# Four of twelve attention items: keys and queries turned in 64x64 tiles of TensorE, with a new order of all operations

## The chip, the core and the metric

The kernel runs on one core of one Trainium2 chip. The metric is device time in microseconds (us) of one launch, as the median of several runs; lower is better. Besides these runs one execution was recorded by the hardware profiler. All rows quoted below come from that recording, which counts time from the first instruction of the program (the span).

## The reference

Two stages follow each other. The first is a gated linear attention with a state per head, in 4 batches of 8 heads, 768 steps and a head dimension of 48:

```python
for t in range(S):
    state = alpha[:, :, t, :, None] * state + np.einsum('bhd,bhe->bhde', k[:, :, t], v[:, :, t])
    y[:, :, t] = np.einsum('bhd,bhde->bhe', q[:, :, t], state)
```

The second takes the 3072 resulting rows x (8 heads of 48 side by side, 384 numbers) through an expert layer with a hidden width of 1024: `np.maximum(x @ w1, x @ w2) @ w_out`. Inputs and output are float32.

## The kernel before

**Tiling.** The sequence is cut into 12 items of 256 steps, three to a batch (`attention(n)`, n = 0 to 11). An item holds all 8 heads, and each partition holds two neighbouring steps. The running products of alpha become sums of logarithms: `ln` (ACT), `su` (pair sums), `cs` (a matmul with a triangular matrix, L605, and sums per block, L610), and the exponentials `inv`, `en`, `ep`, `gg` on ACT. Keys and queries are scaled with these (`ka`, `kt` at L624 and L661; `qi`, `qt` at L629 and L666) into `qkt`, in float16, with a head padded to 64 columns. `vc` casts the values.

**Turning.** The score product needs keys and queries with the head dimension on the partitions. For items 0 to 7 (`TURN`) TensorE turns them: `tk` turns keys, `tq` queries, and a copy of PSUM into SBUF (`ck`, `cq`) follows on DVE or ACT (L488 and L490 are the lines of the helper `cast`). Items 8 to 11 are turned by DMA (`dk`, `dq`, L732). Where an item is not in `T64`, a turn is 8 transposes of 128x128, two heads at once (L692), and keys and queries of the item share one pair of PSUM banks. Where it is in `T64`, each 128x128 block is turned as four blocks of 64x64 that rotate over the four 64x64 tiles of the array, so a turn is 32 transposes, each with 64 columns moving, and `tk` and `tq` take a pair of banks each. Items 0 and 1 are worked in two halves of four heads.

**The rest of an item.** `kv` (L752) makes the contributions to the state in 64x64 tiles with 48 columns moving (32 matmuls; 16 in the last item of a batch). `w`, `t32` and `T` carry the state on. `sc0` and `sc1` (L832) are the scores, 16 matmuls each with 128 columns moving, `pt` masks them on DVE (L840). `yf` (12 matmuls) and `y` (56 or 60, both L877) give the output, and `xe` casts it into `xT`.

**The second stage.** It is rewritten as x @ w2 @ w_out + relu(x @ (w1 - w2)) @ w_out. So at the start `wtp` turns w2, `wd` forms w1 - w2 (DVE, L523), `woc` casts w_out, `mp` multiplies w2 by w_out, `mc` casts that product. For each group g of 256 rows there are then four `h` (6 matmuls each, L943), four relus `r` (L951 on DVE, L953 on ACT), and `o` in two parts a and b for each 128 rows (7 and 4 matmuls, L976). `ev` evicts and `st` stores. `fill` is a matmul on zeros whose result nobody reads (L419).

**What sets the order.** Every operation is an entry of a plan with durations, lags and priorities. But where the string `ORDER` is not empty, `Plan.run` returns `follow()`, which goes through the words of `ORDER`. A word names the operation, the engine (P TensorE, D VectorE, A ScalarE, G GpSimd, S the DMA queue of SyncE) and the PSUM banks:

```python
for word in ORDER.split():
    name, at = word.split(":")
    o = ops[name]
    o.eng = eng[at[0]]
```

Each engine works through its own words strictly in this order and waits where an operand isn't there. Loads go through ten buffers and SyncE's queue in the order of the string. GpSimd operations also wait for the latest VectorE operation before them in the string that is marked `port`.

Of the kernel before, what the change touches and what calls it, by code (L numbers as in the profile page):

```python
# [33 lines left out]
WP = (0.0, 0.0)  # L34
ONACT = ()
FILL = (60, 24.0)
T64 = ()
EARLY = (0, 1)
ORDER = """
fz:D setp1:G ldw20:S setd0:D fill0:P7 lda0.0:S fill31:P lda0.1:S fill32:P fill19:P ldk0.0:S fill6:P setd1:D ldq0.0:S fill5:P fill42:P mask:D fill20:P  # L40
fill38:P lda1.0:S pads0:D fill2:P ldv0.0:S fill36:P pads2:D fill28:P ln0.0:A fill17:P id32:D fill39:P wtp0.0:P6 inv0.0:A su0.0:G lda1.1:S ln0.1:A
cs0.0:P5 fill34:P ldw21:S inv0.1:A su0.1:G fill43:P wtp0.2:P4 gg0.0:A en0.0:A pads1:D fill11:P cs0.1:P ka0.0:G fill1:P fill7:P gg0.1:A fill25:P
ka0.1:D en0.1:A fill18:P kt0.0:D ep0.0:A fill37:P ldwo0:S fill24:P wtc0.0:D kt0.1:G tk0.0:P0 fill27:P wtp0.1:P6 ck0.0:D ln1.0:A qi0.0:D fill33:P
qi0.1:D fill30:P inv1.0:A qt0.0:D su1.0:G tk0.1:P ldw10:S ep0.1:A fill10:P fill8:P ck0.1:D wtc0.2:A tq0.0:P fill35:P qt0.1:D fill13:P cq0.0:A fill29:P
vc0.1:D tq0.1:P fill16:P ln1.1:A vc0.0:D sc0.0:P2 cq0.1:D ldw11:S kv0:P4 su1.1:G pt0.0:D fill22:P cs1.0:P1 fill9:P cs1.1:P gg1.0:A fill12:P en1.0:A
wtc0.1:D sc0.1:P2 ep1.0:A wtp1.1:P0 w0:D ldwo1:S gg1.1:A pt0.1:D T1.0:G fill4:P wtp1.2:P6 T1.1:G t32.1:G y0:P2 woc0.0:A ldk1.0:S w1:D woc0.1:D fill3:P
xe1:A g1:G xe0:D fill41:P wtp1.0:P5 T2.0:G wtc1.1:A ldq1.0:S mp0.1:P4 wtc1.2:A wd0.0:D mp0.2:P0 wtc1.0:A ldv1.0:S wd0.1:D h0.0:P6 en1.1:A mp0.0:P5
r0.0:A wd1.0:D h0.2:P3 lda2.0:S inv1.1:A wd1.1:D h0.4:P6 woc1.0:A lda3.0:S woc1.1:D h0.6:P2 t32.2:G ep1.1:A mp1.0:P r0.6:D r0.2:A ka1.0:G mp1.2:P
ldk2.0:S r0.4:A ka1.1:D mp1.1:P kt1.0:D mc2:A fill15:P qi1.0:D mc0:A tk1.0:P2 ldk3.0:S qi1.1:D fill14:P o0.0a:P6 qt1.0:D kt1.1:G ck1.0:A qt1.1:D
tq1.0:P fill21:P vc1.1:A tk1.1:P vc1.0:D ldq2.0:S cq1.0:D T2.1:G mc1:A kv1:P0 ck1.1:A sc1.0:P4 w2:D tq1.1:P pt1.0:D o0.0b:P T3.0:G ldq3.0:S cq1.1:A  # L50
T3.1:G ln2.0:A t32.3:D yf1:P2 sc1.1:P4 w3:D fill40:P ldv2.0:S su2.0:G inv2.0:A pt1.1:D fill26:P o0.1a:P1 ln3.0:A cs2.0:P7 ka2.0:D y1:P lda4.0:S
en2.0:A su3.0:D ep2.0:A kt2.0:G o0.1b:P xe3:D xe2:A ldv3.0:S ev0.0:D gg2.0:A cs3.0:P0 ev0.1:A h1.0:P6 ka3.0:D gg3.0:A en3.0:A ldk4.0:S tk2.0:P2
qi2.0:D h1.2:P1 r1.0:A g2:G qt2.0:D kt3.0:G inv3.0:A h1.4:P5 ldq4.0:S ep3.0:A ck2.0:D h1.6:P4 r1.2:A r1.4:D tq2.0:P qi3.0:G r1.6:A o1.1a:P1 ldv4.0:S
cq2.0:D vc2.0:A tk3.0:P4 T4.0:G qt3.0:D sc2.0:P2 t32.4:G ck3.0:A kv2:P6 o1.1b:P lda6.0:S T4.1:G w4:D pt2.0:D T5.0:G ln4.0:A tq3.0:P T5.1:G ev1.1:A
lda5.0:S o1.0a:P0 su4.0:G cq3.0:D vc3.0:A yf2:P2 sc2.1:P6 sc3.1:P4 ka4.0:G cs4.0:P1 pt2.1:D ldk5.0:S o1.0b:P en4.0:A ep4.0:A pt3.1:D y2:P ldq6.0:S
gg4.0:A ev1.0:A g4:G kt4.0:G sc3.0:P6 kv3:P4 xe4:D xe5:A ldk6.0:S pt3.0:D inv4.0:A h2.0:P0 qi4.0:G tk4.0:P2 r2.0:A w6:D h2.4:P7 ldq5.0:S t32.7:G
vc4.0:A qt4.0:D h2.2:P6 T7.0:G ln6.0:A h2.6:P0 T7.1:G w7:D ldv6.0:S ck4.0:D T8.1:G tq4.0:P r2.4:A y3:P4 T8.0:G r2.6:D cq4.0:A t32.8:G r2.2:D lda7.0:S
kv4:P0 ln5.0:A sc4.0:P2 o2.0a:P7 w8:D T9.0:D inv5.0:A ldv5.0:S T9.1:D inv6.0:A su6.0:D o2.1a:P6 t32.9:D xe7:A qi6.0:G w9:D xe6:A pt4.0:D ldq7.0:S
o2.0b:P cs6.0:P5 ev2.0:A o2.1b:P su5.0:D gg6.0:A st1.1:S ka6.0:G en6.0:A yf4:P0 ev2.1:D sc4.1:P2 ldv7.0:S h3.0:P7 ep6.0:A pt4.1:D kt6.0:G cs5.0:P6
h3.2:P4 gg5.0:A lda9.0:S r3.0:A qt6.0:D h3.4:P3 r3.2:A qi5.0:G h3.6:P7 r3.4:D vc6.0:A y4:P ldk7.0:S ka5.0:G r3.6:D en5.0:A kv6:P2 ep5.0:A xe9:D  # L60
tk6.0:P4 kt5.0:G xe8:A ldk9.0:S o3.0a:P7 qt5.0:D ck6.0:A w12:D tq6.0:P g5:G ln7.0:A st0.0:S vc5.0:G o3.0b:P cq6.0:D lda8.0:S h4.0:P6 inv7.0:A ev3.0:D
vc7.0:A tk5.0:P0 T10.0:D h4.6:P7 su7.0:D ldq9.0:S T13.0:D cs7.0:P5 t32.13:G h4.2:P4 en7.0:A t32.10:G w13:D tq5.0:P r4.0:A r4.6:D T10.1:G ldq8.0:S
o3.1a:P3 ln9.0:A qi7.0:G ck5.0:D r4.2:A cq5.0:D h4.4:P2 su9.0:G st0.1:S kv5:P6 r4.4:A sc5.0:P0 ldk8.0:S o3.1b:P w10:D gg7.0:A pt5.0:D T11.1:G ep7.0:A
o4.0a:P4 inv9.0:A T11.0:G lda10.0:S ev3.1:A ka7.0:G qt7.0:D yf5:P0 ln8.0:A sc5.1:P2 sc6.0:P6 ka9.0:G o4.0b:P pt5.1:D inv8.0:A st2.0:S o4.1a:P5 kt7.0:G
st1.0:S pt6.0:D ldv9.0:S y5:P T13.1:D kv7:P2 ldq10.0:S g7:G xe10:D xe11:A sc6.1:P6 t32.14:G o4.1b:P pt6.1:D su8.0:G h5.0:P1 ev4.1:A cs9.0:P0 w14:D
st4.1:S h5.6:P5 en9.0:A t32.15:G ldv8.0:S h5.4:P7 T15.1:G w15:D r5.6:A r5.0:D h5.2:P6 T14.0:G ev4.0:A st2.1:S kt9.0:G tk7.0:P2 r5.2:A st3.0:S cs8.0:P1
ck7.0:D tq7.0:P ep9.0:A y6:P4 en8.0:A cq7.0:D ka8.0:G ep8.0:A sc7.0:P2 r5.4:A o5.1a:P6 dk9:S T15.0:G pt7.0:D ln10.0:A qi9.0:G o5.0a:P7 gg8.0:A xe12:D
gg9.0:A vc9.0:A T14.1:G qt9.0:D kt8.0:G o5.1b:P xe13:A yf7:P2 ev5.1:A sc7.1:P4 h6.0:P0 pt7.1:D g8:G dk8:S o5.0b:P r6.0:A h6.6:P6 T16.1:D ev5.0:A
su10.0:D dq9:S h6.2:P0 vc8.0:A t32.16:G r6.6:D qi8.0:G h6.4:P7 inv10.0:A r6.2:D y7:P T16.0:G r6.4:D kv9:P4 qt8.0:D xe14:A kv8:P6 o6.0a:P0 xe15:A w18:D
dq8:S T19.0:G cs10.0:P1 t32.19:G h7.0:P3 gg10.0:A ldk10.0:S en10.0:A qi10.0:D o6.0b:P ldv10.0:S ep10.0:A w19:D T19.1:G o6.1a:P2 r7.0:A st3.1:S  # L70
qt10.0:D ev6.0:A lda11.0:S sc9.1:P4 w16:D sc9.0:P0 h7.2:P3 T17.0:G pt9.0:D ldk11.0:S T17.1:G h7.6:P7 r7.2:A o6.1b:P pt9.1:D r7.6:A ka10.0:G h7.4:P6
st4.0:S ev6.1:A yf8:P0 g10:G r7.4:D sc8.1:P2 kt10.0:G sc8.0:P4 o7.0a:P7 vc10.0:A pt8.0:D o7.1a:P6 pt8.1:D dk10:S o7.0b:P t32.20:D y8:P kv10:P2 xe16:A
xe17:D T20.1:G y9:P4 ka11.0:G ln11.0:A h8.0:P1 xe18:D ev7.0:A su11.0:G o7.1b:P inv11.0:A st7.0:S xe19:A h8.6:P7 ldq11.0:S ev7.1:D h8.2:P0 dq10:S
r8.0:D cs11.0:P6 w20:D r8.2:A h8.4:P1 r8.6:D T21.1:G en11.0:A h9.0:P0 T21.0:G r8.4:D ep11.0:A o8.1a:P7 kt11.0:D gg11.0:A h9.6:P1 T20.0:G dk11:S
qi11.0:G h9.2:P5 r9.6:A h9.4:P4 ldv11.0:S g11:G qt11.0:D t32.21:G o8.1b:P r9.4:A o8.0a:P1 w21:D ev8.1:A r9.2:D r9.0:A t32.22:D yf10:P2 sc10.1:P4
T22.1:D sc10.0:P6 dq11:S T22.0:G o8.0b:P pt10.0:D o9.0a:P0 st6.0:S pt10.1:D vc11.0:G st5.0:S o9.1a:P7 st6.1:S st5.1:S kv11:P4 y10:P w22:D st7.1:S
T23.1:G sc11.0:P4 st8.1:S o9.0b:P xe21:D xe20:A T23.0:G pt11.0:D o9.1b:P h10.0:P6 ev8.0:A ev9.1:D yf11:P2 r10.0:A sc11.1:P4 ev9.0:D h10.2:P7 pt11.1:D
st9.0:S h10.4:P6 r10.2:A h10.6:P1 y11:P r10.6:D o10.0a:P7 xe22:A xe23:D r10.4:A h11.0:P5 o10.1a:P6 r11.0:D h11.6:P5 h11.4:P4 h11.2:P3 r11.4:D o10.1b:P
r11.2:D o10.0b:P ev10.1:D o11.1a:P4 r11.6:D st10.1:S ev10.0:A o11.0a:P6 st8.0:S st9.1:S o11.1b:P o11.0b:P st10.0:S ev11.1:D o11.1c:P7 st11.1:S
ev11.0:D o11.1d:P st11.0:S ev11.11:A st11.11:S  # L80
"""
SHIFT = {}
FIX = {}
# [216 lines left out]
def kernel(  # L300
# [42 lines left out]
    A = {}  # L343
# [85 lines left out]
    def on(key):  # L429
        return "ACT" if key in ONACT else "SP"  # L430

    def add_load(n, which, prio):
# [616 lines left out]
```

## Time and profile before

| | |
|---|---|
| median of 3 runs | 139.66 us (139.44 to 139.73) |
| the profiled execution | 139.41 us, span 137.6 us |
| busy, DVE / ACT / POOL | 99.2 / 74.5 / 69.6 us |
| matmuls and weight loads | 2348 each |
| DMA | 30.76 MB, mean 223 GB/s |

Busy time is the time in which an engine's instructions cover the span; for TensorE (PE) the ends of matmuls are modelled, and matmuls overlap. So a sequence of them is best priced from start to start: the start of a group's first matmul to the start of the next group. In a timeline row the columns are start, length, engine, line, operation, operands and shapes, count, and in brackets the idle time before it with what ended it. An array form such as 64*64 is the part of the array that one matmul uses.

### The profile page before, as it was taken

The numbers are of one execution on the slowest core, as the hardware profiler recorded it, in microseconds if no ns is written. First come the engines' busy times: TensorE is split into PE (matmuls) and PEld (weight loads), VectorE is DVE, ScalarE is ACT, GpSimd is POOL, SyncE is SP. The second block draws the span as 40 slices with busy tenths as digits, with TensorE's granted clock in tenths as the row PEclk, the third lists the DMA queues.
The fourth block names the chain that finished last, engine by engine and source line by source line (L and its number), as shares of the span: only waits on it lengthen the run. The fifth ranks groups of instructions, "written<-read, shape, count | busy, mean of one in ns | idle before, by whom it ended". The sixth has DMA issues, their size and how long they took to land.

```text
span 137.6 us, 5468 instructions
## 1 busy us (share of the span) xinstructions
PE 131.2 (95%) x2348; PEld 94.0 (68%) x2348; DVE 99.2 (72%) x174; ACT 74.5 (54%) x153; POOL 69.6 (51%) x109
## 2 busy tenths in 40 slices
PE   6979989999999999999999999999999999999991
PEld 2445766566786686687867886786767776677770
DVE  7639869789887997787869757876855867575440
ACT  3166365778777779479672596634617460233010
POOL 6054250345698692797679799464545352400000
PEclk9999999999999999999999999999999999999999
DMA  4999999999999999999999999458993869910063
GB/s 89 324 261 315 378 385 332 222 259 274 261 263 257 271 252 237 270 272 254 272 280 287 305 284 161 81 108 144 311 208 100 188 129 149 348 57 5 0 229 114
DMA packets 64680, 30.76 MB, mean 223 GB/s; under 512 B 58896, under 2 KB 63120, under 8 KB 64656
## 3 DMA queue, kind: packets, MB, share of 16 engines
q1 hardware_dynamic: 64656, 30.41, 90.6%
q8 instruction: 18, 0.29, 0.9%
q14 instruction: 6, 0.05, 0.1%
HBM read 23.59 MB, written 4.72 MB: 206 GB/s over the span
## 4 chain that ended last, share of the span: by engine, by line
PE 73%; DMA 13%; SPq 8%; ACT 1%; DVE 1%; issue 1%; POOL 1%; DVEq 0%
PE PS L976 28%; PE PS L943 21%; PE PS L877 10%; DMA ldf<-in_moe_w_out_dram 9%; SPq L448 6%; PE PS L692 5%; DMA ldf<-in_v_dram 4%; PE PS L832 3%; PE PS L752 2%; SPq L470 2%; PE PS L532 2%; PE PS L605 1%; PE PS L419 1%; ACT wo L488 1%; POOL v L492 1%
## 5 line engine op out<-in xcount | busy, mean ns | idle before, releaser
L976 PE MATMUL PS<-wo,g 128*128 128x384 f16 (+1 forms) x200 | 38.3, 320 | 0.1
L943 PE MATMUL PS<-xT,wd 128*128 128x256 f16 x288 | 36.3, 273 | 0.4 <-ACT xT L488 0.2
L840 DVE TENSOR_TENSOR pt<-PS,mask 128x1024 f16<-128x1024 f32 x24 | 28.8, 1219 | 4.5 <-PE PS L832 4.3
L943 PEld LDWEIGHTS <-wd 128*128 128x128 f16 x288 | 26.8, 98 | 6.1 <-DVE wd L523 1.0
L976 PEld LDWEIGHTS <-g 128*128 128x128 f16 x200 | 18.7, 98 | 11.1 <-DVE T L787 0.5
L953 ACT ACTIVATE g<-PS 128x512 f16<-128x512 f32 x27 | 15.9, 595 | 11.9 <-PE PS L943 11.8
L661 POOL TENSOR_TENSOR qkt<-ldf,en 128x768 f16<-128x768 f32 (+1 forms) x11 | 18.3, 1666 | 3.7 <-DVE s L596 1.4
L951 DVE TENSOR_SCALAR g<-PS 128x512 f16<-128x512 f32 x21 | 14.2, 687 | 5.0 <-PE PS L943 4.7
L488 ACT CAST xT<-PS 128x384 f16<-128x384 f32 x14 | 8.0, 594 | 16.1 <-PE PS L877 15.9
L976 PE MATMUL PS<-m,xT 128*128 128x384 f16 (+1 forms) x75 | 15.9, 320 | 0.0
L787 POOL TENSOR_TENSOR T<-w,gg 48x192 f16<-48x192 f32 x20 | 10.4, 520 | 10.4 <-DVE w L812 6.2
L419 PE MATMUL PS<-fz 128*128 128x512 f16 x43 | 14.3, 440 | 1.2 <-DVE fz L416 1.2
L488 ACT COPY outs<-PS 128x384 f32<-128x384 f32 (+1 forms) x16 | 7.5, 469 | 12.4 <-PE PS L976 11.5
L588 ACT ACTIVATE loga<-ldf 128x768 f16<-128x768 f32 (+1 forms) x14 | 10.6, 754 | 5.4 <-DMA ldf<-in_alpha_dram 5.4
L666 DVE TENSOR_TENSOR qkt<-ldf,PS 128x768 f16<-128x768 f32 (+1 forms) x14 | 11.6, 833 | 2.5 <-POOL ldf L629 1.7
L624 POOL TENSOR_TENSOR ldf<-ldf 128x384 f32<-128x384 f32 (+1 forms) x10 | 9.5, 950 | 4.1 <-DMA ldf<-in_k_dram 3.3
L692 PE MATMUL PS<-ident,qkt 128*128 128x128 f16 x128 | 10.4, 219 | 0.2 <-ACT qk L488 0.2
L877 PE MATMUL PS<-pt,v 64*64 64x128 f16 x576 | 10.5, 218 | 0.0
L596 POOL TENSOR_TENSOR s<-loga 128x384 f16<-128x384 f16 (+1 forms) x9 | 6.8, 750 | 7.3 <-ACT loga L588 6.6
L812 DVE TENSOR_TENSOR w<-PS,t 112x192 f32<-112x192 f32 x16 | 5.7, 355 | 6.4 <-PE PS L752 3.5
L692 PEld LDWEIGHTS <-qkt 128*128 128x128 f16 x128 | 8.5, 98 | 2.6 <-DVE qkt L666 0.9
L877 PEld LDWEIGHTS <-v 64*64 64x64 f16 x576 | 8.5, 107 | 2.0 <-issue 1.6
(77 smaller groups left out, 184.3 us busy)
## 6 DMA issues: line engine op xcount, KB each, us to landing
ldf<-in_k_dram SPq DMA_DIRECT2D x12, 384.0 KB, 6.1
ldf<-in_q_dram SPq DMA_DIRECT2D x12, 384.0 KB, 6.5
ldf<-in_v_dram SPq DMA_DIRECT2D x12, 384.0 KB, 5.8
out_dram<-outs SPq DMA_DIRECT2D x23, 192.0 KB, 3.7
ldf<-in_alpha_dram SPq DMA_DIRECT2D x10, 384.0 KB, 5.9
ldf<-in_moe_w_dram SPq DMA_DIRECT2D x4, 768.0 KB, 7.9
ldf<-in_moe_w_out_dram SPq DMA_DIRECT2D x2, 768.0 KB, 10.0
ldf<-in_alpha_dram SPq DMA_DIRECT2D x4, 192.0 KB, 5.3
```

The lines of the kernel that those rows point to most:

```text
L419: plan.add(f"fill{i}", {"PE": 0.21}, lambda eng: nc.tensor.matmul(bank(fb), lhsT=fz[:, 0:128], rhs=fz, start=True, stop=True, skip_group_c ...
L488: nc.scalar.copy(out=out, in_=in_)
L588: nc.scalar.activation(out=A["loga", n][:, hd].rearrange("p h j d -> p (h j d)"), in_=A["ld", n, "a"][:, hd].rearrange("p h d -> p (h d)") ...
L661: e.tensor_mul(out=hjd(qkts[i3], 1)[:, hd], in0=A["ld", n, "k"][:, hd].rearrange("p h (j d) -> p h j d", j=2), in1=f.unsqueeze(2).to_broad ...
L666: nc.vector.tensor_mul(out=hjd(qkts[i3], 0)[:, hd], in0=A["ld", n, "q"][:, hd].rearrange("p h (j d) -> p h j d", j=2), in1=f.unsqueeze(2). ...
L692: nc.tensor.transpose(t[:, a, r, j, :], src[:, j, r, :], ident16)
L840: nc.vector.tensor_mul(out=t.rearrange("p u r c -> p (u r) c"), in0=A["sc", n, hf].rearrange("p u (r c) -> p (u r) c", r=2), in1=mask.rear ...
L877: nc.tensor.matmul(dst, lhsT=lhsT, rhs=rhs, start=(x, u) not in begun, stop=done and ends[x, u] == i, skip_group_check=True)
L943: nc.tensor.matmul(t[:, i], lhsT=wd16[:, s, (f + i) * 128 : (f + i + 1) * 128], rhs=xT[:, s, a0 : a0 + W], start=(s == 0), stop=(s == 2), ...
L951: nc.vector.tensor_relu(o, i)
L953: nc.scalar.activation(out=o, in_=i, func=ACTF.Relu)
L976: nc.tensor.matmul(A["op", t0, c], lhsT=lhsT, rhs=rhs, start=(part == 0 and j == 0), stop=(part == 1 and j + 1 == len(todo[1])))
```

## The change

`T64` goes from empty to items 4, 5, 6 and 7. For these four, `tk` and `tq` take the other branch of the code above, which already stands in the file, and the copies `ck` and `cq` read two half banks instead of whole ones. In the built program TensorE has 2545 matmuls instead of 2348: 192 more from the turns, and 48 fills instead of 43. `ORDER` is replaced as a whole. The lags of the loads in the plan are changed too; since `ORDER` isn't empty, no number of the plan is used.

```diff
-T64 = ()
+T64 = (4, 5, 6, 7)
...
 ORDER = """
-fz:D setp1:G ldw20:S setd0:D fill0:P7 lda0.0:S fill31:P lda0.1:S fill32:P fill19:P ldk0.0:S fill6:P setd1:D ldq0.0:S fill5:P fill42:P mask:D fill20:P
...
-xe1:A g1:G xe0:D fill41:P wtp1.0:P5 T2.0:G wtc1.1:A ldq1.0:S mp0.1:P4 wtc1.2:A wd0.0:D mp0.2:P0 wtc1.0:A ldv1.0:S wd0.1:D h0.0:P6 en1.1:A mp0.0:P5
-r0.0:A wd1.0:D h0.2:P3 lda2.0:S inv1.1:A wd1.1:D h0.4:P6 woc1.0:A lda3.0:S woc1.1:D h0.6:P2 t32.2:G ep1.1:A mp1.0:P r0.6:D r0.2:A ka1.0:G mp1.2:P
-ldk2.0:S r0.4:A ka1.1:D mp1.1:P kt1.0:D mc2:A fill15:P qi1.0:D mc0:A tk1.0:P2 ldk3.0:S qi1.1:D fill14:P o0.0a:P6 qt1.0:D kt1.1:G ck1.0:A qt1.1:D
-tq1.0:P fill21:P vc1.1:A tk1.1:P vc1.0:D ldq2.0:S cq1.0:D T2.1:G mc1:A kv1:P0 ck1.1:A sc1.0:P4 w2:D tq1.1:P pt1.0:D o0.0b:P T3.0:G ldq3.0:S cq1.1:A
...
+setp1:G lda0.0:S ln0.0:A fz:D setd0:D fill0:P7 ldk0.0:S lda0.1:S fill44:P fill8:P fill15:P ldw20:S pads0:D id32:D ldq0.0:S setd1:D fill34:P fill10:P
...
+fill42:P fill30:P fill13:P ep1.1:A xe0:A wtc1.2:A h0.0:P3 mp0.2:P5 wd0.1:D r0.0:A lda2.0:S lda3.0:S wd1.0:D wtc1.1:D wd1.1:D h0.2:P2 h0.4:P3 woc1.1:A
+h0.6:P0 r0.2:A woc1.0:D mp1.2:P ldk2.0:S ka1.1:D ka1.0:D kt1.0:D kt1.1:D mp1.1:P r0.6:A r0.4:A qi1.0:D qt1.0:D ldq2.0:S mp1.0:P mc2:A ldq3.0:S mc1:A
+tk1.0:P2 tk1.1:P qi1.1:G mc0:A o0.0a:P5 tq1.0:P qt1.1:D tq1.1:P ck1.0:D cq1.1:D vc1.1:G vc1.0:A kv1:P0 ck1.1:A cq1.0:A t32.2:G ldk3.0:S w2:D T3.1:D
+t32.3:D w3:D ln2.0:A o0.0b:P ev0.0:A sc1.0:P2 pt1.0:D ldv2.0:S o0.1a:P6 T3.0:G yf1:P0 sc1.1:P4 pt1.1:D ln3.0:A inv3.0:A lda4.0:S fill27:P su2.0:G
...
+T8.0:G ka6.0:G tk4.0:P0 y3:P4 r2.6:D ln5.0:A ep6.0:A tq4.0:P2 o2.1a:P6 xe7:A xe6:D o2.0a:P5 h3.0:P4 t32.8:D qi6.0:D qt6.0:D su5.0:G T8.1:G ck4.0:A
+vc4.0:A cq4.0:D st0.0:S ldq5.0:S vc6.0:A r3.0:A kv4:P0 sc4.0:P2 w8:D t32.9:D o2.0b:P ev2.0:A pt4.0:D T9.0:G T9.1:G o2.1b:P w9:D h3.2:P7 kt6.0:G
...
+ka5.0:D tk6.0:P2 r3.6:A r3.4:D y4:P en5.0:A su7.0:G T10.1:D kv6:P0 xe9:D st1.0:S ldq8.0:S st0.1:S o3.0a:P7 xe8:A h4.0:P5 inv7.0:A ep5.0:A ck6.0:A
+t32.10:G w12:D t32.13:D kt5.0:D o3.0b:P r4.0:A h4.2:P4 w13:D tk5.0:P0 ck5.0:A qi7.0:G ev3.0:D st3.0:S r4.2:D tq6.0:P2 cq6.0:D cs7.0:P7 en7.0:A ep7.0:A
+h4.4:P5 r4.4:A gg7.0:A T10.0:G qi5.0:G qt5.0:D vc5.0:G ldk9.0:S o3.1a:P4 st2.0:S ka7.0:D kt7.0:G qt7.0:D h4.6:P3 r4.6:A ldq9.0:S o3.1b:P kv5:P0 w10:D
+T11.0:G tq5.0:P2 ev3.1:A cq5.0:A sc6.0:P6 pt6.0:D o4.0a:P5 ln9.0:A sc5.0:P0 pt5.0:D T11.1:G yf5:P2 sc5.1:P6 o4.0b:P ev4.0:A T13.1:G inv9.0:A ln8.0:A
+lda10.0:S ldk8.0:S ldv9.0:S vc7.0:G o4.1a:P4 kv7:P0 ldq10.0:S pt5.1:D y5:P xe11:A inv8.0:A T13.0:G g7:G t32.14:G w14:D t32.15:D sc6.1:P6 o4.1b:P
...
+h8.0:P5 inv11.0:A w20:D h9.0:P0 kt11.0:G dk11:S ev7.1:A h8.2:P7 r8.2:A t32.21:G g11:G r9.0:A h9.2:P6 ep11.0:A h8.4:P4 T21.0:D st4.1:S w21:D ldv11.0:S
+r9.2:D T22.0:G h8.6:P7 r8.6:A qi11.0:G r8.0:D h9.4:P6 r9.4:A T21.1:D qt11.0:D dq11:S h9.6:P5 o8.0a:P7 r9.6:D r8.4:A sc10.0:P0 T20.1:G T20.0:G yf10:P2
...
```

Across the whole string some operations change engine as well: relus on ACT go from 27 to 34 and on DVE from 21 to 14, evictions on ACT from 16 to 20, copies of turned tiles on ACT from 7 to 9.

## The prediction

> **What bounds the kernel now.** First the totals and the slices of the page:
>
> ```profile
> PE 131.2 (95%) x2348; PEld 94.0 (68%) x2348; DVE 99.2 (72%) x174; ACT 74.5 (54%) x153; POOL 69.6 (51%) x109
> PE   6979989999999999999999999999999999999991
> PEclk9999999999999999999999999999999999999999
> PE 73%; DMA 13%; SPq 8%; ACT 1%; DVE 1%; issue 1%; POOL 1%; DVEq 0%
> ```
>
> TensorE (PE) is covered in every slice after the start, at the full granted clock, and 73% of the chain that ended last is PE; the other engines have room. Next, where the chain leaves PE:
>
> ```profile
> 11.99 12.71 DMA ldf<-in_moe_w_out_dram
> 24.72 0.84 ACT wo L488
> 25.60 2.11 PE PS L532 x12
> ```
>
> Up to 24.7 us the loads set the pace: `wo1` lands, ACT casts half of it, and mp1 starts at 25.60. From the end of mp1 (27.55) to the last matmul (134.70) the chain is nearly all PE. So I split the program at mp1. Read word by word, both orders hold the same operations of PE before mp1 and the same after it, apart from fills: five fills behind mp1 before (15, 14, 21, 40, 26), four now (27, 35, 11, 3). The part behind mp1 can then be priced as a sum.
>
> **Prices**, from start to start in the PE timeline:
>
> ```profile
> 60.87 0.86 PE L877 MATMUL PS<-pt,v 64*64 64x128 f16 x48
> 61.56 0.34 PE L877 MATMUL PS<-qk,T 48*64 48x128 f16 x12
> 61.73 0.44 PE L752 MATMUL PS<-v,qkt 64*64 64x48 f16 x32
> 62.10 0.62 PE L692 MATMUL PS<-ident,qkt 128*128 128x128 f16 x8
> 62.56 0.65 PE L976 MATMUL PS<-m,xT 128*128 128x384 f16 x3
> ```
>
> A wide turn (8 transposes) takes 62.56 - 62.10 = 0.46, in rows between wide neighbours 0.45. `y` with 60 matmuls takes 61.73 - 60.87 = 0.86. Where a wide matmul follows `y` directly (33.84 to 34.81) it is 0.97, so leaving the small tiles costs 0.11. Six `h` matmuls take 0.65 between their like and 0.74 before a small-tile group (97.52 to 98.26): entering costs 0.09. A stay in small tiles thus costs 0.20. `kv6` above takes 0.37 - 0.11 = 0.26 for 32 matmuls. With these prices the old order behind mp1 sums to 105.2 us; measured 107.15, so 1.95 are waits and misfits, 0.16 of it the pipeline's end.
>
> **The turns of items 4 to 7.** Eight turns of 0.45 go, eight turns of 32 small transposes come. No row shows these. Below: `kv6`, the same array form and rotation over four tiles with 48 columns moving, 0.26 (8.1 ns each). Above: `sc`, 128 columns moving, 16 in 0.22 (13.8 ns each), so 32 in 0.44. At 64 columns, nearest `kv`, a straight line between them gives 9.3 ns, 0.30 a turn. I take 0.30: 8 x (0.45 - 0.30) = 1.2 us saved; by the ends 1.5 or 0.1. The copies from PSUM carry as many elements as before (DVE 0.69, ACT 1.01); should the half banks halve DVE's pace, 0.7 more on four copies falls beside `o` and `h` matmuls with 0.6 us of slack (below), so I cost it at nothing, 0.1 each if that cover is gone.
>
> The Trainium skill, "TensorEngine Tiling (Array Packing)", section Instruction Overhead, speaks against this change: about 60 cycles go with each matmul, one of 1 column takes as long as one of 60, and a dimension already small is not to be tiled. Taken as 25 ns an instruction (60 cycles at the 2.4 GHz of "TensorE: Matmul & The Clock Gate") without overlap between tiles, an estimate from these pages would be 0.80 a turn and +2.8 us for the change; the row of `kv6`, 8.1 ns each, says that rotating tiles don't pay that here.
>
> **Stays in small tiles.** Counted in the strings behind mp1: 22 before, 25 now. `tk4 y3 tq4`, `tk6 y4`, `kv5 tq5 sc6`, `tk7 y6 tq7` sit beside small-tile work and cost no switch; `tk5 tq6` stands alone, `sc6`/`sc5` are parted by an `o`, and early on `kv1` and `sc1.0` are parted. +0.60 in all, 0.20 of it before the turns.
>
> **From mp1 to h2.0, the step that loses.** In the new string DVE does `wtc1.1` between the two halves of `wd1`:
>
> ```profile
> 22.64 1.83 DVE L523 TENSOR_TENSOR wd<-ldf 128x768 f16<-128x768 f32 x2 [0.24 <-DMA ldf<-in_moe_w_dram]
> 24.72 0.56 DVE L490 CAST wo<-ldf 128x768 f16<-128x768 f32 x1 [0.25 <-DMA ldf<-in_moe_w_out_dram]
> 26.06 0.36 DVE L624 TENSOR_TENSOR ldf<-ldf 128x192 f32<-128x192 f32 x1
> ```
>
> Both halves end at 24.47 here. With 0.68 (the row of w2T casts on DVE) between, the second ends at 25.15, the cast `woc1.0` at 25.7, `h0.6` at 25.9, and mp1 starts there: +0.3. The start can't make up for it: `wo1` is the thirteenth load in both strings, with the same twelve ahead of it (alpha and k of item 0 now ahead of `w20`), and six more fills there lie in about 3 us of idle PE.
>
> Then item 1. Behind the arrival of k1 (26.05) DVE now does all of `ka1.1 ka1.0 kt1.0 kt1.1 qi1.0`: 0.36 + 0.36 + 0.56 + 0.56 + 0.37 = 2.2, to 28.25. Only then may GpSimd do `qi1.1` (0.76, the 128x192 row of L624), to 29.1, then `qt1.1` on DVE 0.55, to 29.7. PE is at `tq1.1` at 29.2 by the sum: wait 0.5. Queued behind it on PE stands `kv1`, and for that wait `w2`, `T3` and `yf1`. Some loads stand later in the string. By the landing times of the same places in the old one, k3 lands at 38.2 instead of 34.7, and `kt3` still ends by 41.0 with `tk3` due at 41.6; v3 lands at 45.5 instead of 42.7, and `vc3` ends at 46.4 with `kv3` due at 47.5. No wait there. At `h2.0`, DVE has `pt2.1 pt3.1 xe5` in a row (1.22 + 1.22 + 0.59) and is late by 0.15.
>
> Against these the old stretch had its own: 0.17 at `o0.0a`, 0.29 at `h2.0`, 0.10 of crumbs. Sum to `h2.0`: 0.3 + 0.5 + 0.15 - 0.56 - 0.22 (a fill) + 0.20 (the stay) = **+0.4**.
>
> **From h2.0 to the end.** I held the queues against the PE sum, item by item, each by the rows. `cq4`: DVE has 0.59 + 0.35 + 0.55 + 0.95 + 0.69 behind `y3`, PE 0.3 + 0.1 + 1.14 + 1.14 + 0.66 + 0.1 + 0.27: slack 0.6. `tk6` 0.5, `yf4` 0.15, `cq5` (ACT, 1.01) 0.2; `yf5` is late by 0.1 (`T11` behind `kt7`, 1.81 on GpSimd), `y5` by 0.15 (three `pt` in a row). The DMA turns start later (`dk9` near 83 to 84 instead of 81.9), but `sc9` and `yf8` still have 2 us. `h8.0`, `h9.0`, `y10`, `y11` and the tail have 0.1 to 1. What goes:
>
> ```profile
> 111.18 5.56 DMA ldf<-in_v_dram
> 116.79 0.83 POOL v L492
> 117.67 0.34 PE PS L752 x11
> ```
>
> `ldv11` stood behind a DMA turn and held `kv11` by 0.2; now it is issued two words earlier and `vc11` is on ACT. At `o2.0a` 0.32 goes, whose cause I couldn't find; I count half. So 0.25 - 0.36 = -0.1. What is late next after `kv11` is nothing but PE itself.
>
> Sum: +0.4 (to `h2.0`) - 1.2 (turns) + 0.4 (two stays) - 0.1 = **-0.5 us**, on 139.41 of the profiled execution (span 137.6 and 1.8 around it, which stay): 138.9. The median is 0.25 above that execution, so **139.1**.
>
> **Rivals.** *Small transposes cost like scores* (slower): 0.44 a turn, place `tk4` to `tq7`, +1.1, 140.3. It decides from 0.36 a turn, where the gain is gone. For: rotating tiles pay by columns, and 64 is above 48. Against: 64 columns are half of 128. Chance 0.14.
>
> *One queue of the new order is late* (the tight spots at `tq1.1`, `yf4`, `cq5`, `y5`; ACT has 7 us more work than before): a wait of 1 us more, 140.1. For: ACT carries seven more relus; a late cast delays its whole queue. Against: ACT's 54%. Chance 0.11.
>
> *PE's instructions don't arrive in time.* 394 more of them, most between 46 and 89 us: I count 256 per 4.7 us there on average. In the trace the packets of the instruction queue (18 of them, 16 KB) follow each other at 4.5 to 4.6 us where they are closest in a row. A cycle of 5 would add about 1 us: 140.1. Against: 256 went by in 3.0 us around 104 without more than 0.1 lost. Chance 0.05.
>
> *The gain is swallowed* (no change): the loss before `h2.0` is 0.9 instead of 0.4, because `tq1.1` or `y1` wait longer: 139.6. Chance 0.14.
>
> *The start loses nothing* (`wtc1.1` fits in while DVE waits for w1, GpSimd's half is quicker): 138.4 and below. Chance 0.10.
>
> **Numbers.** Forecast 139.1 with 0.46 (138.6 to 139.35). About 0.2% (0.28 us) can be told from no change. Faster: 0.46 + 0.10 = 0.56; same 0.15; slower 0.29 (the first three rivals, 0.30, less what of them ends near 139.6). Range 138.1 to 140.4: below, turns at 0.26 and no loss at the start; above, turns at 0.44 or one lost microsecond.
>
> **What will show it.** Starts in the PE timeline: small turns 0.26 to 0.35 for 32; mp1 at 25.9 instead of 25.60; a gap of 0.5 before the last transposes of item 1; `h2.0` some 0.4 to 0.7 later (it now also has `cs6` ahead of it, 0.27); the last matmul ending near 134.2. `kv11` without a wait for v11. I am wrong if small turns take over 0.36, if PE shows gaps over 0.5 between 48 and 120 us, or if mp1 starts after 26.3.

## The result, and the profile after

| | before | after |
|---|---|---|
| median | 139.69 us (139.44 to 140.24, 4 runs) | 144.36 us (143.99 to 144.78, 4 runs) |
| profiled execution, span | 139.41, 137.6 us | 144.69, 142.8 us |

The ratio is 1.0329 (95% interval 1.0281 to 1.0377): the changed kernel is 3.3% slower, where 0.4% faster was forecast. Here and below, ratios compare only the runs within 1.5% of the fastest of their kernel, while medians and ranges take in all of them. The page of after, its totals, slices, queue of instructions and chain:

```profile
PE 132.7 (93%) x2545; PEld 92.9 (65%) x2545; DVE 93.1 (65%) x158; ACT 82.4 (58%) x166; POOL 68.4 (48%) x112
...
PE   6989998999999969976999999999999999998991
...
PEclk9999999999999999996899999999999999999999
...
q8 instruction: 20, 0.33, 1.0%
...
PE 74%; DMA 9%; SPq 8%; issue 3%; DVE 3%; POOL 0%; ACT 0%; POOLq 0%; DVEq 0%
```

Three things differ from before. PE has two holes in the middle: the digit 6 at 50 to 54 us, and 7 and 6 at 61 to 68 us. The granted clock falls to 0.6 and 0.8 in the 19th and 20th slice, right behind the second hole (in windows of 1 us it is 0.50 from 66 to 69 us). And "issue", time in which PE waits for nothing that the profile shows, goes from 1% of the chain to 3%. What PE waited for behind mp1 (line, what ended the wait, total, times, longest):

```profile
PE PS L976 <- issue: 2.2, 1, 2.2
PE PS L699 <- issue: 1.2, 1, 1.2
PE PS L943 <- DVE xT L490: 0.9, 2, 0.7
PE PS L692 <- DVE qkt L666: 0.3, 1, 0.3
```

The first two have no operand as their cause. PE's timeline around them (start, length, engine, line, operation, shapes, count):

```profile
52.03 0.39 PE L699 MATMUL PS<-ident,qkt 64*64 64x64 f16 x27
53.64 0.25 PE L699 MATMUL PS<-ident,qkt 64*64 64x64 f16 x5 [1.23 <-issue]
```

```profile
61.71 0.45 PE L699 MATMUL PS<-ident,qkt 64*64 64x64 f16 x32
61.98 0.84 PE L877 MATMUL PS<-pt,v 64*64 64x128 f16 x48
62.66 0.34 PE L877 MATMUL PS<-qk,T 48*64 48x128 f16 x12
62.83 0.44 PE L752 MATMUL PS<-v,qkt 64*64 64x48 f16 x32
65.42 0.96 PE L976 MATMUL PS<-m,xT 128*128 128x384 f16 x3 [2.15 <-issue]
66.17 1.49 PE L976 MATMUL PS<-wo,g 128*128 128x384 f16 x4
67.45 1.49 PE L943 MATMUL PS<-xT,wd 128*128 128x256 f16 x6
```

`tq4` stops between its 27th and 28th transpose, in the middle of one operation whose input is complete. `o3.0a` starts 2.22 later than `kv6` allows. Then four `o` matmuls take 1.49 and six `h` 1.49, at full clock 0.81 and 0.82.

**Where the 5.2 us of the span come from.** mp1 starts 0.39 earlier (25.21 for 25.60). Behind it, PE's own work by the prices of the prediction, with the measured 0.27 a small turn, sums to 104.14 instead of 105.2: -1.06. Waits and misfits grow from 1.94 to 8.56: +6.62. Of the 8.56, 4.04 are stops without a cause in the profile (`tq4` 1.41, `o3.0a` 2.22, `o5.1a` 0.28, `h2` 0.13), 1.69 the slow clock behind the second one, 1.26 two waits for `xT`, 0.43 the wait at `tq1.1`; the rest, 1.1, is in small pieces as before. This holds for the profiled execution. Its mean granted clock is 0.988; in the other three runs of after it is 0.997 to 1.0, and they take 143.99 to 144.78 all the same. So they show little of the slow clock, and what they lose in its place no trace shows.

### The profile page after: what moved, and what is told of

It reads as the page before. It is cut to its first block, busy times and chain, and to the rows that moved or that the text cites. A ratio compares the mean times of both kernels' runs of the same rounds, so it can differ in the third digit from the quotient of the medians.

```text
span 142.8 us, 5868 instructions
## 1 busy us (share of the span) xinstructions
PE 132.7 (93%) x2545; PEld 92.9 (65%) x2545; DVE 93.1 (65%) x158; ACT 82.4 (58%) x166; POOL 68.4 (48%) x112
## 4 chain that ended last, share of the span: by engine, by line
PE 74%; DMA 9%; SPq 8%; issue 3%; DVE 3%; POOL 0%; ACT 0%; POOLq 0%; DVEq 0%
PE PS L976 32%; PE PS L943 21%; DMA ldf<-in_k_dram 9%; PE PS L877 9%; SPq L448 5%; PE PS L832 4%; PE PS L752 2%; PE PS L699 2%; SPq L470 2%; PE PS L692 2%; PE PS L605 1%; SPq L467 1%; DVE xT L490 1%; PE PS L419 1%; DVE qkt L661 1%
## 5 line engine op out<-in xcount | busy, mean ns | idle before, releaser
L953 ACT ACTIVATE g<-PS 128x512 f16<-128x512 f32 x34 | 19.8, 596 | 14.6 <-PE PS L943 14.3
L661 POOL TENSOR_TENSOR qkt<-ldf,en 128x768 f16<-128x768 f32 (+1 forms) x9 | 15.5, 1727 | 10.0 <-ACT gg L649 4.8
L488 ACT COPY outs<-PS 128x384 f32<-128x384 f32 (+1 forms) x20 | 9.2, 462 | 14.1 <-PE PS L976 14.0
L629 POOL TENSOR_TENSOR ldf<-ldf,inv 128x384 f32<-128x384 f32 (+1 forms) x10 | 9.1, 915 | 11.5 <-DVE ldf L629 9.8
L787 POOL TENSOR_TENSOR T<-w,gg 48x192 f16<-48x192 f32 x18 | 9.3, 518 | 7.2 <-DVE t L799 3.6
L951 DVE TENSOR_SCALAR g<-PS 128x512 f16<-128x512 f32 x14 | 9.5, 687 | 4.4 <-PE PS L943 4.3
L596 POOL TENSOR_TENSOR s<-loga 128x384 f16<-128x384 f16 (+1 forms) x9 | 7.8, 868 | 5.3 <-ACT loga L588 1.6
L490 DVE COPY outs<-PS 128x384 f32<-128x384 f32 x5 | 2.8, 552 | 11.2 <-PE PS L976 11.1
L490 DVE CAST xT<-PS 128x384 f16<-128x384 f32 x10 | 5.9, 591 | 6.3 <-PE PS L877 4.4
L976 PEld LDWEIGHTS <-xT 128*128 128x128 f16 x75 | 6.4, 98 | 5.3 <-issue 2.3
```

The source lines that it names most:

```text
L488: nc.scalar.copy(out=out, in_=in_)
L490: nc.vector.tensor_copy(out=out, in_=in_)
L661: e.tensor_mul(out=hjd(qkts[i3], 1)[:, hd], in0=A["ld", n, "k"][:, hd].rearrange("p h (j d) -> p h j d", j=2), in1=f.unsqueeze(2).to_broad ...
L951: nc.vector.tensor_relu(o, i)
L953: nc.scalar.activation(out=o, in_=i, func=ACTF.Relu)
L976: nc.tensor.matmul(A["op", t0, c], lhsT=lhsT, rhs=rhs, start=(part == 0 and j == 0), stop=(part == 1 and j + 1 == len(todo[1])))
```

## The experiments

A stop is called here after the operation in which it falls or which it follows: "at `o2.0a`" means between the start of `o2.0a` and the start of PE's next operation.

**Theory.** PE's instructions come in blocks. In the trace queue q8 moves 20 packets of 16 KB (before: 18). Counted by the program (a weight load and a matmul each, 24 more loads for the float32 transposes of the start, and the few waits between them), the stops stand at the same place of a block of 256: `tq4` at instruction 1731, `o3.0a` at 2243, 512 later. And before's unexplained 0.32 at `o2.0a` stands at 1731 as well, in this row of before, which takes 1.13 where others of its kind take 0.81:

```profile
53.60 1.13 PE L976 MATMUL PS<-wo,g 128*128 128x384 f16 x4
```

So I took 195 past each multiple of 256 as the end of a block, and PE waits there if the next block hasn't come. **Rivals:** dense small transposes cost by themselves, wherever blocks end; or the new order's queues are late.

All the shifts below make the same edit: a fill in the idle start is cut short and followed by matmuls of 8 columns, each of which is two instructions. Everything behind the start keeps its operations and moves against the blocks.

```diff
-            plan.add(f"fill{i}", {"PE": 0.21}, lambda eng: nc.tensor.matmul(bank(fb), lhsT=fz[:, 0:128], rhs=fz, start=True, stop=True,
...
+            def e_fill(eng, i=i):
+                more = 0 if i in (27, 35, 11, 3) else 2
+                w = 512 - 64 * more
+                nc.tensor.matmul(bank(fb, w), lhsT=fz[:, 0:128], rhs=fz[:, 0:w], start=True, stop=True, skip_group_check=True)
+                for _ in range(more):
+                    nc.tensor.matmul(bank(fb, 8), lhsT=fz[:, 0:128], rhs=fz[:, 0:8], start=True, stop=True, skip_group_check=True)
```

**a_shift**: after, 88 such matmuls (+176 instructions).

> The changed kernel; each of the 44 fills ahead of mp1 is 384 columns instead of 512, followed by two matmuls of 8 columns on the same zeros, so TensorE has 176 instructions more, all in the start, for about the same time. No result changes. Fetch theory: TensorE's instructions come in blocks of 256, the next block is fetched when the block before it has been entered, and takes about 4.4 us; in the changed kernel blocks end just behind the dense stretches tk4-y3-tq4, tk6-y4-kv6, tk7-y6-tq7. Shifting the ends by 176 instructions takes them apart: the gaps at tq4, kv6 and o5.1a go, the clock stays full, 139.0 to 140.5. Rival, the small turns or the density of the new order cost this much wherever the blocks end: 143.5 to 145. Rival, a limiter lowers the clock for dense small tiles: the clock still dips near 65 us.

Measured: 141.07 us (139.69 to 143.96, 7 runs), ratio to before 1.0088 (1.0031 to 1.0144), 0.6 above the range expected; its profiled execution has a span of 139.2 and the clock at 1.0. The same stretch of PE:

```profile
61.37 0.84 PE L883 MATMUL PS<-pt,v 64*64 64x128 f16 x48
62.04 0.34 PE L883 MATMUL PS<-qk,T 48*64 48x128 f16 x12
62.21 0.44 PE L758 MATMUL PS<-v,qkt 64*64 64x48 f16 x32
62.59 0.66 PE L982 MATMUL PS<-m,xT 128*128 128x384 f16 x3
63.09 0.81 PE L982 MATMUL PS<-wo,g 128*128 128x384 f16 x4
63.74 0.82 PE L949 MATMUL PS<-xT,wd 128*128 128x256 f16 x6
```

The same operations in the same order, and `o3.0a` starts 0.38 after `kv6` instead of 2.59. The stop in `tq4` is gone too. 3.3 us come back by adding instructions.

**a_ctrl**: after, 16 such matmuls (+32), as a control.

> The changed kernel; the first 16 fills are 448 columns instead of 512 and followed by one matmul of 8 columns, 32 instructions more in the start. No result changes. Control for the shift: by the fetch theory the block ends move by 32 and still fall in or behind the same dense stretches, the sum of gaps by a count with 4.4 us a block is about the same (6.8 instead of 6.7), so 143.5 to 145. If tiny matmuls among the fills help or hurt by themselves, it is as fast or slow as the shift by 176.

Measured: 146.88 us, ratio 1.0553 (1.0492 to 1.0614), more than expected. The count with 4.4 us a block (between the 4.24 and 4.55 from block end to block end in after) puts the waits at `cs6.0` (1.4), `kv6` (1.3), `tq7.0` (1.0) and `h8.0` (2.3); of these only a sum was on record ahead of the run. The trace has them at `cs6.0` 1.37, in `kv6` 1.27, at `tq7.0` 0.64 and in `kv10`, one operation ahead of `h8.0`, 2.02. (The profile puts the one at `cs6.0`, which ends at 49.84, down to ACT, whose instruction had ended at 49.05.) Two of them in the timeline, and the clock row of the page:

```profile
63.70 0.29 PE L758 MATMUL PS<-v,qkt 64*64 64x48 f16 x16
65.10 0.31 PE L758 MATMUL PS<-v,qkt 64*64 64x48 f16 x16 [1.11 <-issue]
...
108.01 0.41 PE L758 MATMUL PS<-v,qkt 64*64 64x48 f16 x31
110.27 0.21 PE L758 MATMUL PS<-v,qkt 64*64 64x48 f16 x1 [1.84 <-issue]
```

```profile
PEclk9999999999999999999999999999998699999999
```

`kv6` now breaks after 16 of 32 matmuls, `kv10` before its last one. The clock falls behind the stop of 2.0 us, and not behind those of 1.3 and 1.4. With fewer extra matmuls than a_shift the kernel is 5.8 us slower, so it is the place and not the number.

**a_wide**: after with wide turns (`T64 = ()`).

> The changed kernel with its order, but T64 empty: all turns are wide again, 192 matmuls fewer. No result changes. Fetch theory: with 384 instructions fewer between 50 and 90 us the blocks last longer, the gaps nearly vanish (1.2 us by the count), turns cost 8 x 0.18 more: 139.5 to 141. If the order itself (other engines, load order) is what costs, it stays at 143 or more.

Measured: 142.28 us, ratio 1.0199 (1.0153 to 1.0245): slower than I expected. The profiled execution (143.19, the slowest of its runs) starts mp1 at 26.9, because `w1`'s first half landed at 21.6; it keeps the waits for `xT` (0.84, 0.42) and at `tq1.1` (0.40), and has smaller ones at `h2.4`, `kv5` and `o5.1b` (0.35 to 0.61). Only the first of these is a block's end. Behind `kv5` the profile has `tq5` waiting for DVE's `w` (0.5), and behind `o5.1b` the next operation waiting for ACT's `xT` (0.3). The wait behind `kv5` comes with this edit: a wide `tq5` uses the pair of banks of `tk5`, and the order puts `kv5` into one of them. So the order without the small turns is 2.0% slower than before, where the whole change is 3.3% slower, in several pieces, and 0.6 us of it come from the edit.

**b_small**: the old order with the four items' turns in 64x64 tiles, keys and queries in halves of one pair of banks as the old order wants it.

```diff
-T64 = ()
+T64 = (4, 5, 6, 7)
...
-tb = [Buf("A"), Buf("A")]
+tb = [tpb, tpb]
...
-t = pair(tb[a]).bitcast(FP16)[:, :, 0:512].rearrange("p x (r j m) -> p x r j m", r=NP, j=2)
+t = pair(tb[a]).bitcast(FP16)[:, :, 512 * a : 512 * a + 512].rearrange("p x (r j m) -> p x r j m", r=NP, j=2)
```

> The kernel before with its order, and T64 = (4, 5, 6, 7); keys and queries of an item share one pair of banks, each in its half, since the order names only one pair. No result changes. Fetch theory: turns save 8 x 0.18 less the switches, but four blocks now end within dense stretches (tk4, kv4, o3.0a, sc7.0), gaps of 4 to 7 us: 142.5 to 146. If the new order is the cause and small turns are harmless: 139.2 or below.

Measured: 144.82 us (142.42 to 146.21), ratio 1.0301 (1.0214 to 1.0389); the profiled execution (146.21, the slowest of its runs) has stops at the four places named ahead, `tk4` (1.19), `kv4` (0.75), `o3.0a` (0.87) and `sc7.0` (1.97), and behind the last of them the clock at 0.50 from 88 to 90 us. The 0.50 at `cs8` is something else: the profile has `tq7` waiting there for the cast of the keys on DVE, presumably since with this edit each of the two banks holds a part of both turns, where before has the keys in one and the queries in the other. The turns alone, in an order whose queues had no such waits, cost by the ratios about as much as the whole change. The two halves of the change don't add up, since each also moves the ends of the blocks. By itself this fits the rival "small transposes cost" as well; the next run parts them.

**b_align**: b_small with 72 short matmuls in the start (+144 instructions).

> The old order with small turns for items 4 to 7 (as b_small), and 144 instructions more in the start: 36 fills of 384 columns, each followed by two matmuls of 8 columns. No result changes. Fetch theory: the count of gaps falls from 7.2 to 2.6 us, so from 144.8 to 139.8 to 141. If small turns are dear in the old order for another reason (they share one pair of banks here): 143 or more.

Measured: 141.07 us, ratio 1.012 (1.0075 to 1.0164). By the two ratios 1.8% come back with the same transposes. Stops of 0.85 (`o2.1a`) and 1.27 (`tk5.0`) are left, and the wait of 0.52 for the cast at `cs8`: this shift doesn't move every end into a harmless place.

**e_rate**: before, with 1280 matmuls of 64x64x64 on zeros behind the first fill, rotating over the four tiles. It measures the blocks by themselves: PE has more work than instructions.

```diff
+if i == 0:
+    for _ in range(320):
+        for x, u in ((0, 0), (1, 1), (0, 1), (1, 0)):
+            o = 64 * x
+            nc.tensor.matmul(PS[64 * u : 64 * u + 64, 6 + x, 0:64], lhsT=fz[o : o + 64, 0:64], rhs=fz[o : o + 64, 0:64],
+                             start=True, stop=True, skip_group_check=True)
```

> The kernel before; behind its first fill TensorE does 1280 matmuls of 64x64 tiles with 64 columns on zeros, rotating over the four tiles (2560 instructions, ten blocks of 256). No result changes. If instructions arrive freely, the 1280 take 8 to 9 ns each warm, 11 us (up to 22 where the clock isn't up yet). Fetch theory: 256 instructions per 4.2 to 4.6 us however short they are, so 10 blocks take some 40 to 46 us, with a gap of about 3 us in every 128 matmuls, and the packets of the instruction queue stand 4.2 to 4.6 us apart.

Measured: 181.74 us, in one execution. PE's timeline, and the windows (length, busy time of PE, PEld, DVE, ACT and POOL, granted clock, DMA share, GB/s):

```profile
1.74 2.97 PE L425 MATMUL PS<-fz 64*64 64x64 f16 x222
8.75 1.92 PE L425 MATMUL PS<-fz 64*64 64x64 f16 x128 [4.04 <-issue]
13.30 1.92 PE L425 MATMUL PS<-fz 64*64 64x64 f16 x128 [2.63 <-issue]
19.77 1.93 PE L425 MATMUL PS<-fz 64*64 64x64 f16 x128 [4.55 <-issue]
26.24 1.92 PE L425 MATMUL PS<-fz 64*64 64x64 f16 x128 [4.54 <-issue]
31.34 1.92 PE L425 MATMUL PS<-fz 64*64 64x64 f16 x128 [3.18 <-issue]
34.80 1.92 PE L425 MATMUL PS<-fz 64*64 64x64 f16 x128 [1.53 <-issue]
38.52 1.92 PE L425 MATMUL PS<-fz 64*64 64x64 f16 x128 [1.81 <-issue]
```

```profile
10.00:20.00 10.00, 2.82 (x196) 2.56 (x191) 0.20 (x1) 0.00 (x0) 0.66 (x1) 0.50 1.02 332
20.00:30.00 10.00, 3.62 (x255) 3.35 (x248) 0.00 (x0) 0.00 (x0) 0.00 (x0) 0.50 0.85 242
30.00:40.00 10.00, 5.32 (x368) 5.05 (x371) 0.00 (x0) 0.00 (x0) 0.00 (x0) 0.50 0.02 5
```

Bursts of exactly 128 matmuls, 256 instructions, each ended by a wait without a releaser. From burst to burst it takes 4.55 to 6.47 us while loads run (DMA share 0.85 to 1.02) and 3.46 to 3.72 when they have ended (0.02). So PE is served one block per 3.5 to 6.5 us here, and the slow ones go with DMA load beside them. That the load makes them slow isn't shown: c_bad, below, has a block in 2.9 us at a DMA share of 1.01.

**a_space**: after, with `o2.1a` put ahead of `tq4.0` and `o3.0a` ahead of `tk6.0`, so that 1.1 us of wide matmuls (14 instructions) go between the dense groups; no shift.

```diff
-tk4.0:P0 y3:P4 r2.6:D ln5.0:A ep6.0:A tq4.0:P2 o2.1a:P6
+tk4.0:P0 y3:P4 r2.6:D ln5.0:A ep6.0:A o2.1a:P6 tq4.0:P2
...
-tk6.0:P2 r3.6:A r3.4:D y4:P en5.0:A su7.0:G T10.1:D kv6:P0 xe9:D st1.0:S ldq8.0:S st0.1:S o3.0a:P7
+o3.0a:P7 tk6.0:P2 r3.6:A r3.4:D y4:P en5.0:A su7.0:G T10.1:D kv6:P0 xe9:D st1.0:S ldq8.0:S st0.1:S
```

> The changed kernel with two words of its order moved: o2.1a ahead of tq4.0, o3.0a ahead of tk6.0, so that long matmuls stand within the dense stretches. No instruction more or less. Fetch theory by the count with 4.4 us a block: the gap at tq4.0 (1.4) goes, that behind kv6 shrinks from 2.2 to 1.0 to 1.4 and is then too short to lower the clock (it stayed full behind gaps of 1.4 in other runs), so 3 us less: 140.5 to 142.5. If the gaps belong to the small turns themselves: no change, 143.5 or more.

Measured: 142.25 us, ratio 1.0176 (1.0125 to 1.0226), clock 1.0. The stops at `tq4` and `kv6` shrink to 0.38 and 0.59. There are 0.81 at `h2.4` and 1.24 at `o5.1a`, where the profile of after has 0.13 and 0.28; ahead of `h2.4` the two programs are the same, so the size of a stop differs between executions. Two words moved take 2.1 us away, again without touching the turns.

**a_best**: a_shift, the four late fills out (27, 35, 11, 3), `ka1.1` on GpSimd, and `y11` and `h10.6` moved up so that the casts `xe23` and `xe22` stand ahead of other reads of `xT`.

```diff
-ka1.1:D ka1.0:D
+ka1.1:G ka1.0:D
...
-o9.1b:P ev9.1:A st9.1:S o9.0b:P ev9.0:D st9.0:S h10.0:P1 r10.0:D y11:P h10.4:P5 h10.6:P4 xe23:A xe22:D h11.0:P7 h10.2:P6
+o9.1b:P ev9.1:A st9.1:S h10.0:P1 r10.0:D h10.6:P4 y11:P xe23:A xe22:D o9.0b:P ev9.0:D st9.0:S h11.0:P7 h10.4:P5 h10.2:P6
```

> The changed kernel shifted by 176 instructions in the start, and three edits of its order: the four fills behind mp1 left out (0.2 us each), ka1.1 on GpSimd beside ka1.0 on VectorE (tq1.1 waits 0.4 less), and y11 between o9.1b and o9.0b, so that xe22 and xe23 stand ahead of the h matmuls of group 10 that read other columns of xT (0.8 less at h11.0). No result changes. By these sums 141.07 - 0.86 - 0.3 - 0.7: 138.5 to 139.7. If the xT wait is a real dependence on y11, the gap of 0.8 stays and the time is 139.5 to 140.5.

Measured: 140.57 us (140.15 to 140.79), ratio 1.0081 (1.0053 to 1.0109): missed. The move of `y11` did what it should (`h11.0` loses 0.13 instead of 0.84). But the fills had stood in waits of others, which now show: `sc1.1` to `cs2.0` 0.52, `kv2` to `tk3.0` 0.43, `sc2.0` 0.28. Two block ends also stop PE, by 0.55 and 0.64, at 70.98 and 76.35 us.

**c_good and c_bad**: the cleanest pair. The order of before, `T64 = (6,)` with the edit of b_small, and in the start 100 short matmuls (+200 instructions) or 52 (+104), chosen by the count as the best and a bad place.

> The order of before, only item 6's two turns in 64x64 tiles, and 200 more PE instructions (100 matmuls of 8 columns) in the idle start, placed so that by the count no block of PE's instructions ends in a dense stretch (count of gaps 0; at 4.7 us a block 0.5). Theory (blocks of 256 instructions fetched in 4.2 to 4.7 us): two turns at 0.27 instead of 0.45 save 0.36 less one more stay in small tiles 0.2, and the 0.32 at o2.0a goes: 138.8 to 139.3, 0.2 to 0.5 under before. Rival (the small turns cost their time whatever the alignment, a fifth of what four items cost per item and more): 140.2 or more.

> The same as c_good in every operation after the start, but 104 instead of 200 more PE instructions (52 matmuls of 8 columns) in the idle start. Theory: the ends of blocks fall at kv3 (gap 1.0 to 1.4), o3.0a (2.1 to 2.6) and y9 (2.3 to 2.8), and the clock drops after the last two (1 to 1.6 each): 144.5 to 147. Rival (alignment of blocks doesn't matter, or the extra matmuls themselves cost): the same as c_good or, with fewer extra matmuls, a little below it.

Measured: c_good 139.25 us (138.53 to 139.95, 12 runs), ratio 0.9989 (0.9961 to 1.0018); c_bad 141.48 us (140.98 to 143.54, 6 runs), ratio 1.0159 (1.0116 to 1.0202). PE behind `kv6` and `tk5` in c_good, then in c_bad, and `y9` of c_bad:

```profile
61.76 0.50 PE L705 MATMUL PS<-ident,qkt 64*64 64x64 f16 x32
62.19 0.66 PE L982 MATMUL PS<-m,xT 128*128 128x384 f16 x3
62.68 0.81 PE L982 MATMUL PS<-wo,g 128*128 128x384 f16 x4
```

```profile
61.57 0.49 PE L705 MATMUL PS<-ident,qkt 64*64 64x64 f16 x32
62.00 0.34 PE L982 MATMUL PS<-m,xT 128*128 128x384 f16 x1
63.43 0.50 PE L982 MATMUL PS<-m,xT 128*128 128x384 f16 x2 [1.10 <-issue]
...
104.37 0.80 PE L883 MATMUL PS<-pt,v 64*64 64x128 f16 x41
105.94 0.30 PE L883 MATMUL PS<-pt,v 64*64 64x128 f16 x7 [0.77 <-issue]
```

Two programs with the same operations behind the start differ by 2.2 us, and the stops stand at two of the three operations named ahead, `o3.0a` and `y9`. Their size was wrong: 1.28 and 1.00 instead of 2.1 to 2.8, `kv3` none, and so no fall of the clock. In c_bad 3.5 and 2.9 us lie between the ends of these blocks, not 4.4. In c_good one stop of 0.28 is left, at `y9`, and `kv11` waits 0.49 for GpSimd's cast of the values. What it gains by its two small turns is no more than this measurement can tell.

**c_seven and c_32**: item 7 in place of item 6 with +200; and before itself with +32, nothing else.

> As c_good, but item 7 instead of item 6 in 64x64 tiles, 200 more PE instructions. Theory: count of gaps 0, two turns save 0.36 less 0.2 for a stay, 0.32 at o2.0a goes: 138.8 to 139.3. Rival as for c_good: 140.2 or more.

> The kernel before with 32 more PE instructions (16 matmuls of 8 columns) in the idle start and nothing else. Theory: the gap of 0.32 at o2.0a (a block end there) goes, and by the count one of 0.5 to 0.7 at h2.0 comes, where before has 0.29 by other causes: 139.0 to 139.5, hardly to be told from before. Rival (more matmuls in the start cost or nothing changes): the gap at o2.0a stays.

Measured: c_seven 139.96 us, ratio 1.0036 (1.0007 to 1.0066), 0.7 above the range expected. It has no stop at a block's end, as counted; its 0.52 at `cs8.0` is again `tq7` waiting for the cast on DVE. c_32 140.48 us, ratio 1.0077 (1.0052 to 1.0101): the stop at `o2.0a` went, and one of 0.88 came at `h2.0`, five of whose six matmuls run before it. The place was as counted, the time 1 us more than expected; 0.47 of the profiled execution's waits are at `o0.0a`, where `tq1.0` waits for DVE's `qkt`, which the shift doesn't explain. No version was measurably faster than before.

**All stops together.** Counted in the same way, the profiles of before, of after and of the eleven variants in this section other than e_rate have 23 waits of PE behind mp1, of over 0.15 us, that the profile puts down to "issue". Every one stands at instruction 194 or 195 past a multiple of 256, and so do the stops at `cs6.0` of a_ctrl and `o2.0a` of before, for which it names other engines. No other wait of that length does. The trace also has the times of q8's packets: in after they start at 51.12 and 62.87, end 1.2 later, and PE goes on at 53.64 and 65.42. In all 25 cases PE goes on 1.2 to 1.7 us after such a packet has ended. So these stops are waits for the next block, wherever the small transposes lie.

## Why the prediction was wrong, point by point

**The price of a small turn: right.** 0.30 was predicted, 0.27 is measured (61.71 to 61.98 above), 8.4 ns from start to start. The rival of dear small turns falls. The stays in small tiles stood at 25; with the turns they give -1.06 on the sum of PE, where the steps of the prediction had -0.8.

**From mp1 to h2.0: about right.** `tq1.1` waits 0.43 (0.5 predicted). The start was missed: mp1 came 0.39 earlier where 0.3 later was forecast. `wtc1.1` does delay the second half of `wd1`, for which PE waits 0.59 at 24.55, but the loads landed some 0.6 earlier (ACT's cast of `wo1` starts at 24.15, in before at 24.72). mp1 started at 25.21 in the profile of after and at 25.5 to 26.9 in those of its variants, as the first loads land; 25.9 lay within that.

**The late queues from h2.0 on: mostly right, two missed.** `kv11` lost its wait. What I had held against the sum was no more than 0.1 late, but `h8.0` lost 0.42 and `h11.0` 0.84. The second, PE's row in after:

```profile
127.08 1.48 PE L943 MATMUL PS<-xT,wd 128*128 128x256 f16 x12
129.24 2.03 PE L943 MATMUL PS<-xT,wd 128*128 128x256 f16 x17 [0.68 <-DVE xT L490]
```

`h11.0` reads what `xe22` and `xe23` write, and both start at 128.60, when the last matmul of `h10.6` has ended. `h10.6` reads other columns of `xT`; the casts wait for it all the same (the profile names that matmul as what ends their wait), presumably since they stand behind it in the string and write the same tile. In a_best, with `y11` and the casts moved up, they start with the end of `y11`, and `h11.0` loses 0.13.

**The step that failed: "PE's instructions don't arrive in time", given 0.05 and "about 1 us".** The sum has nothing for it. In the profiled execution it cost 4.0 us of stops and 1.7 us of clock behind the longest; together 5.7, of which before had 0.3, against 6.6 by which all waits grew. The sign that the prediction named for its own failure, gaps over 0.5 us between 48 and 120, is what the profile showed. Three things were wrong in it:

- *The average.* "I count 256 per 4.7 us there on average" against a cycle of 4.5 to 4.6 seemed to fit. But a wait depends on the single block: 256 instructions of `tk6 y4 kv6` and what lies around them went in the 1.9 us of `h3.6` to `kv6`, and a surplus before them can't be saved up beyond what is already fetched.
- *The clock.* That a stop of 2 us would be followed by 3.4 us at half the clock was in no rival.
- *The counter-evidence.* "256 went by in 3.0 us around 104 without more than 0.1 lost" is no block. By the count, before has block ends at 99.50 and 103.81 us, in the middle of that dense stretch, so its instructions were split between a block of 4.3 us and one of 10.2. c_bad has the stretch in one block: it took 2.9 us and stopped PE for 1.00. In after, from end to end between 49 and 66, blocks that stopped PE took 4.2 to 4.6, in e_rate beside the loads of the start up to 6.5.

And two hints were at hand. The 0.32 at `o2.0a`, "whose cause I couldn't find", was the end of a block. And the plan in the code has the constants `BLOCK = 256`, `REFILL = 4.4` and `AHEAD = 63.0`, close to what the runs show (256, 4.2 to 4.6 in this stretch, ends at 195, which is 256 - 61); I had set the plan's numbers aside as unused. The plan counts 0.35 instructions more per operation than the program has, so that by its count the fetch lies elsewhere (the ninth end in `kv6` instead of at `o3.0a`). Whether the new order was searched for with that count, and lost by it, I could not find out.

The Trainium skill has the rule: "Runtime: NRT & Kernel Launch", section Instruction fetch mechanics, says that engines fetch 256 instructions (16 KiB) at a time on a DMA queue of their own, and that crossing a block's end is mostly hidden, because instructions are issued slower than the blocks come. The first half agrees with the packets of q8 and the bursts of 128 matmuls; the second fails here, where 256 instructions of rotating 64x64 tiles take 1.1 us (128 x 8.4 ns) and a block 2.9 to 6.5.

**What stays open.** The size of a single stop: the count names the operation, mostly, and is up to twice too high or low, since it takes every block for 4.4 us where those that stopped PE took 2.9 to 5.4; what sets that time isn't known. What the three runs of after without a clear fall of the clock lost in its place. And the rest of a_shift against before (1.2 us): 1.26 at `h8.0` and `h11.0` and 0.43 at `tq1.1` would explain it, but 1.4 us of waits at `tk4` and `sc6.0` (block ends) and `o5.1b` (ACT's `xT`) stand against the -1.06 of PE's own work, and those I didn't part.

## What to carry to other kernels

When a change adds many short instructions to an engine, divide its program into blocks of 256 and set the time of each block of its own, not the average, against the blocks' interval in the trace. The mark is a wait that ends with "issue", in the middle of an operation, just behind a packet of the instruction queue. A few harmless instructions in an idle stretch move all the ends behind them, so try several such shifts before calling a change bad, and compare two versions each at its own good shift. A saving of 1 us from denser work can be lost where the blocks of instructions for it come 4 us apart.

## What the runs showed of the hardware

- PE's instructions came in blocks of 256 here, and PE went on 1.2 to 1.7 us after a block's packet had ended. From one block to the next it took 3.46 to 3.72 us with the DMA engines all but idle (share 0.02, e_rate), 2.9 to 5.4 in this kernel from 48 us on where PE had to stop, and up to 6.47 beside the loads of e_rate's start.
- Behind the three stops of 2.0 to 2.2 us (after, a_ctrl, b_small) the granted clock was 0.5 for some 3.4 us; behind those of 1.1 to 1.4 it stayed at 1.0. "TensorE: Matmul & The Clock Gate" of the Trainium skill, section What's actually happening, has the clock fall after an idle window of about 3.4 us; here a shorter stop was enough.
- Transposes of 64x64 that rotate over the four tiles start every 8.4 ns at full clock (32 in 0.27 us); matmuls of that shape at the clock of 0.5 every 13 ns (e_rate, 128 started within 1.68 us).
